# Two buffers for the splitting of weights in an mLSTM and feed-forward kernel, and a new place for the row gates' buffers

## The chip, the cores and the metric

The kernel runs on one core of a Trainium2 chip. The metric is the device time of one execution in microseconds (us). The engines are named as in the profile: PE (TensorE, matrix products), PEld (its weight loads), DVE (VectorE), ACT (ScalarE), POOL (GpSimd) and SP (SyncE, which here issues all DMAs).

## The reference

An mLSTM attention over B = 4, H = 8, S = 768, D = 40, whose output feeds a feed-forward layer of 320 to 2048 to 320 over 3072 tokens. Cut to what matters:

```python
for t in range(S):                                   # per batch and head
    m_new = max(f[t] + m, i[t])
    f_stab, i_stab = exp(f[t] + m - m_new), exp(i[t] - m_new)
    m = m_new
    C = f_stab * C + i_stab * outer(v[t], k[t])
    n = f_stab * n + i_stab * k[t]
    y[t] = sigmoid(o[t]) * (C @ q[t]) / max(abs(n @ q[t]), 1)
...
h = x @ w_in                                         # x: y as (3072, 320)
g = where(h >= 1, h, where(h <= -1, 0, (h + 1)**2 / 4))
out = g @ w_out
```

## The kernel before, in words

The sequence is cut into 6 chunks of 128 steps, so there are 24 pairs n of a chunk and a batch. For each pair a lower triangular matrix of decays A is built (an affine select on POOL, exponentials on ACT), multiplied into the scores k·q (DVE), and multiplied by v on PE; from the second chunk on, a carried state C is added (DVE tiles `hv`). The result y is transposed by PE into `xh` and `xl`, two parts of x.

The feed-forward layer works on 4 pairs (512 tokens) at a time, in 6 groups j, each with 16 slices fc of 128 of the 2048 hidden columns. For each slice `mm1` runs 8 products into one of two PSUM banks `psh`; ACT reads the bank into a tile `r` (a relu, then a square in place) and DVE reads the bank once more and finishes r (`scalar_tensor_tensor`, "the read r" in what follows). Only after that read may the bank be written for the slice after the next. `mm2` multiplies r into four banks `pso` two slices later. From j = 1 on, r is split into `gh` and `gl`, and w_out is split too.

The weights come as 64-bit numbers and are turned into 32-bit numbers on the chip, in 16 pieces: 8 of w_in (two slices each, 128 x 768 numbers, "in0" to "in7") and 8 of w_out (128 x 640, "out0" to "out7"), in the order in0, in1, out0, in2, out1 and so on. Raw words are loaded into `wraw`, which has two buffers; the load of the piece after the next is issued when the piece in its buffer has been read. `words` then does five steps: the *magnitude* (ACT, from wraw into `mg`), the *sign* (DVE, from wraw into the upper halves of the output), the *low half* (POOL, from wraw into the lower halves), the *clamp* (DVE, mg in place), and the *combine* (DVE, mg into the output). For w_in the output is the tile `win`, which is split further: its *high part* goes to `wh` (ACT) and its *rest* to `wl` (DVE). For w_out the output is a tile `ow`, and it is split only from j = 1 on (into `oh` and a second `ow`).

The time before the first feed-forward products is called the front; its order is written out by hand, one token a step (STEPS), and each engine keeps it. `c` in it converts in0, `d` its rest; `Lf`, `b` and `g1` load the row gates of four chunks, find their maxima and sum them on DVE (tiles `fi_r`, `m_r`, `fi_b`, `m_b`). Behind the front a planner, which plays the program through with estimated times while it is built, sets the order on each engine: it takes what is ready by its estimates and comes first in the program. A tile whose buffer is still in use isn't ready. What the code gives it for the pieces is this:

```python
while nw < min(len(W_ORDER), DUE(fc)):      # DUE(fc) = 3 + fc, group j = 0 alone
    split_next()
...
with behind((m, "act"), (m, "dve")):        # in split_next: not ahead of the last copy of xh, xl
    for _ in convert(*W_ORDER[nw]):
        pass
if nw + 2 < len(W_ORDER):
    load_w(*W_ORDER[nw + 2])
```

The memory is handed out in pools. `stage` holds wraw, win and mg; it is given back when the last piece is converted, and `late` (the tiles v3 and m3 of later pairs) takes its place. `gate` holds what only the front needs; at its end `gates.close()` gives it back, and `mo` (tiles r, gh, gl) takes its place. `mid` stays to the end.

Of the kernel before, what the change touches and what calls it, by code (L numbers as in the profile page):

```python
# [7 lines left out]
F32 = mybir.dt.float32  # L8
# [11 lines left out]
L = 128  # L20
# [3 lines left out]
P = 128  # L24
# [3 lines left out]
NSEQ = B * H  # L28
# [70 lines left out]
def mlstm_ffn_kernel(ctx, tc, qk, qn, vk, og, fi0, fi, fib, w_in, w_out, cst, out):  # L99
# [9 lines left out]
    stage = stages.enter_context(tc.tile_pool(name="stage", bufs=2, side="right"))  # L109
# [7 lines left out]
    mid = ctx.enter_context(tc.tile_pool(name="mid", bufs=1))  # L117
    gates = ExitStack()
    gate = gates.enter_context(tc.tile_pool(name="gate", bufs=1))
# [61 lines left out]
    mb = {}  # L181

    def load_batch():
        mb["row"] = mid.tile([NSEQ, 2, 4 * L], F32, name="fi_r")
        nc.sync.dma_start(mb["row"], fi[:, :, L:5 * L])
        mb["fi"] = mid.tile([P, 2, L], F32, name="fi_b")
        nc.sync.dma_start(mb["fi"], fib)

    def batch_maxima():
        m = mid.tile([NSEQ, 4 * L + 1], F32, name="m_r")  # L190
        nc.vector.tensor_copy(m[:, 0:1], carry)
        nc.vector.tensor_tensor_scan(out=m[:, 1:], data0=mb["row"][:, 0, :], data1=mb["row"][:, 1, :], initial=m[:, 0:1],
                                     op0=ALU.add, op1=ALU.max)
        nc.vector.tensor_copy(carry, m[:, 4 * L:])
        mb["m"] = mid.tile([P, L + 1], F32, name="m_b")
        for c in range(4):
            nc.sync.dma_start(mb["m"][c * NSEQ:(c + 1) * NSEQ], m[:, c * L:(c + 1) * L + 1])
# [174 lines left out]
    def words(out, raw):  # L372

        n = raw.shape[1] * raw.shape[2] // 2
        hi = raw.rearrange("p k (f w) -> p (k f) w", w=2)[:, :, 1]
        quarter = raw.rearrange("p k f -> p (k f)").bitcast(U16).rearrange("p (f w) -> p f w", w=4)
        out = out.rearrange("p k f -> p (k f)").bitcast(I32)
        halves = out.bitcast(U16).rearrange("p (f w) -> p f w", w=2)  # L380
        mg = stage.tile([P, n], F32, name="mg", bufs=1)
        nc.scalar.activation(mg, hi.bitcast(F32), AF.Abs, scale=65536.0)
        nc.vector.tensor_scalar(out=halves[:, :, 1], in0=quarter[:, :, 3], scalar1=0x8000, scalar2=None,
                                op0=ALU.bitwise_and)

        nc.gpsimd.tensor_scalar(out=halves[:, :, 0], in0=quarter[:, :, 1], scalar1=1 / 8192, scalar2=-4095.5 / 8192,
                                op0=ALU.mult, op1=ALU.add)
        nc.vector.tensor_scalar_max(mg, mg, TINY)
        nc.vector.scalar_tensor_tensor(out=out, in0=mg.bitcast(I32), scalar=3, in1=out,
                                       op0=ALU.logical_shift_left, op1=ALU.bitwise_or)  # L390

    def split(hi, lo, w):
        nc.scalar.copy(hi, w)
        yield
        nc.vector.tensor_tensor(out=lo, in0=w, in1=hi.bitcast(F32), op=ALU.subtract)
# [14 lines left out]
    def convert(kind, i):  # L410
        raw = raws.pop((kind, i))
        if kind == "in":
            sl = slice(2 * i * P, 2 * (i + 1) * P)
            w = stage.tile([P, 3, 2 * P], F32, name="win", bufs=1)
            words(w, raw)
            yield
            yield from split(wh[:, :, sl], wl[:, :, sl], w)
        else:
            of[i] = ow.tile([P, 656], F32, name="ow")[:, :2 * DM].rearrange("p (k e) -> p k e", k=2)
            words(of[i], raw)  # L420
            if 2 * i >= PLAIN_FC:
                yield
                yield from split_out(i)

    def split_out(i):
        w = of.pop(i)
        ol[i] = ow.tile([P, 656], F32R, name="ow")[:, :2 * DM].rearrange("p (k e) -> p k e", k=2)
        yield from split(oh[:, 2 * i:2 * i + 2, :], ol[i], w)
# [359 lines left out]
    def split_next(m="x"):  # L788
        nonlocal nw
        if nw < len(W_ORDER):  # L790
            with behind((m, "act"), (m, "dve")):
# [4 lines that stand above are left out]
            nw += 1  # L796
# [5 lines left out]
    for what in STEPS.split():  # L802
        n = int(what[1]) if what[1:2].isdigit() else 0
        hh = int(what[2:] or 0)
        if what == "Lg":
            first_gates()
        elif what == "Lf":
            load_batch()
        elif what == "Lc":
            nc.sync.dma_start(cs_t, cst[0:120, P:])  # L810
# [14 lines left out]
        elif what[0] == "g":  # L825
            if n:
                batch_sums()
            else:
                run(gate_sums(n))
        elif what[0] == "b":  # L830
            batch_maxima()
        elif what[0] == "k":
            run(gate_tail(n))
        elif what[0] == "h":
            gate_exps(n)
        elif what[0] == "A":
            add_sums(n)
        elif what[0] == "E":
            exponents(n)
        elif what[0] == "p":  # L840
            first_sums()
        elif what[0] == "v":
            scale1(n)
        elif what[0] == "o":
            sigmoid(0)
        elif what[0] == "x":
            decay(n, hh)
        elif what[0] == "c":
            rest = convert(*W_ORDER[nw])
            next(rest)  # L850
            load_w(*W_ORDER[nw + 2])
            nw += 1
        elif what[0] in "ed":
            next(rest, None)
        elif what[0] == "w":
            heat = int(what[1:])
        elif what[0] in "uytz":
            if what[0] == "u":
                mains[n] = main(n)
            next(mains[n])  # L860
# [110 lines left out]
```

## Time and profile before

| | |
|---|---|
| median of 3 runs | 518.3 us (518.03 to 519.18) |
| the profiled execution | 517.97 us, its span 516.2 us |
| PE busy | 490.7 us (95%) |
| DVE busy | 343.0 us (66%) |
| ACT busy | 289.1 us (56%) |
| POOL busy | 135.9 us (26%) |
| mean granted clock of PE | 0.979 |
| DMA | 51.48 MB, mean 100 GB/s |

The profile is of one execution. Its views are the page (busy time of each engine), the waits (which engine waited for whom, total, times and longest), the chain that ended last (followed back from the last instruction, step by step to what released it), the time line (start, duration, engine, line, operation, output and inputs with their shapes, and in brackets the idle time before it and what ended it), and the stretches (busy time of each engine in a stretch of time, the clock granted to PE as a share of full speed, and the use of the DMA engines). Nearly all instructions carry line 82 or 85, that of a helper, so they are told apart by their tiles.

### The profile page before, as it was taken

How to read it: one execution, taken by the hardware profiler on the slowest of the kernel's cores; microseconds unless marked ns; L12 is line 12 of the kernel's file. 1: busy time of each engine (PE TensorE's matmuls, PEld its weight loads, DVE VectorE, ACT ScalarE, POOL GpSimd, SP SyncE). 2: the span in 40 equal slices, each digit the busy share in tenths (PEclk: the TensorE clock that was granted, in tenths of full speed). 3: DMA queues.
4: the chain of work that ended last, by engine and by line, in shares of the span. 5: the costliest groups of instructions: out<-in, count | busy, mean ns of one | idle time of the engine just before them, and what ended most of it. 6: DMA issues, size and time to landing. Idle time of an engine off the chain costs nothing.

```text
span 516.2 us, 8817 instructions
## 1 busy us (share of the span) xinstructions
PE 490.7 (95%) x3396; PEld 419.4 (81%) x3399; DVE 343.0 (66%) x621; ACT 289.1 (56%) x560; POOL 135.9 (26%) x136
## 2 busy tenths in 40 slices
PE   8985999889898999999999998999999999999996
PEld 3763877778677989988889988889888889988986
DVE  4789896679758776759696657756756745444332
ACT  4525884436087555676645567555377554455553
POOL 2324531343433333323142314403230210000000
PEclk8987999979999999999999999999999999999999
DMA  8868664364441303323223423113522000010001
GB/s 227 257 183 307 161 189 138 115 193 150 131 146 40 107 27 96 118 66 111 65 78 83 133 80 118 68 53 96 170 81 77 16 1 1 0 52 1 1 2 51
DMA packets 29646, 51.48 MB, mean 100 GB/s; under 512 B 10060, under 2 KB 19940, under 8 KB 29604
## 3 DMA queue, kind: packets, MB, share of 16 engines
q1 hardware_dynamic: 29604, 50.92, 32.4%
q8 instruction: 27, 0.44, 0.4%
q14 instruction: 15, 0.12, 0.1%
HBM read 46.80 MB, written 4.04 MB: 98 GB/s over the span
## 4 chain that ended last, share of the span: by engine, by line
PE 85%; DVE 6%; ACT 5%; DMA 3%; issue 1%; SPq 0%; ACTq 0%; DVEq 0%
PE pso L82 33%; PE psh L82 33%; PE psa L82 15%; ACT Abc L82 1%; PE pso L85 1%; DMA raw<-in_qk 1%; ACT L82 1%; PE psa L85 1%; DVE ow L82 1%; DMA wraw<-in_w_in 1%; PE psh L85 1%; ACT r L82 1%; DVE win L82 1%; DMA out<-r 1%; ACT sig L82 0%
## 5 line engine op out<-in xcount | busy, mean ns | idle before, releaser
L82 ACT ACTIVATE r<-psh,half 128x512 f32<-128x512 f32 x96 | 65.4, 685 | 111.7 <-PE psh L82 111.4
L82 DVE SCALAR_TENSOR_TENSOR r<-psh,r 128x512 f32<-128x512 f32 x96 | 65.8, 686 | 71.5 <-ACT r L82 71.3
L82 PE MATMUL psh<-xh,wh 128*128 128x512 f32 x288 | 104.3, 418 | 6.7 <-DVE r L82 6.1
L82 PE MATMUL pso<-oh,gh 128*128 128x320 f32 x320 | 100.6, 317 | 2.4 <-ACT gh L82 2.1
L82 PE MATMUL psh<-xh,wl 128*128 128x512 f32 x288 | 99.8, 401 | 0.0
L82 PE MATMUL pso<-ow,gh 128*128 128x320 f32 x320 | 99.2, 312 | 0.0
L82 PE MATMUL pso<-oh,gl 128*128 128x320 f32 x320 | 94.0, 311 | 1.6 <-DVE gl L82 1.6
L82 DVE TENSOR_TENSOR gl<-r,gh 128x512 fp32r<-128x512 f32 x80 | 62.2, 779 | 40.5 <-ACT gh L82 40.4
L82 ACT CAST gh<-r 128x512 fp32r<-128x512 f32 x80 | 49.4, 618 | 51.0 <-DVE r L82 50.4
L82 PEld LDWEIGHTS pso<-oh,gh 128*128 128x128 f32 x320 | 60.1, 188 | 7.4 <-ACT gh L82 2.5
L82 PEld LDWEIGHTS psh<-xh,wl 128*128 128x128 f32 x288 | 55.2, 192 | 13.1 <-DVE wl L85 0.4
L82 PEld LDWEIGHTS psh<-xh,wh 128*128 128x128 f32 x288 | 51.8, 194 | 15.2 <-DVE r L82 6.8
L82 PEld LDWEIGHTS pso<-ow,gh 128*128 128x128 f32 x320 | 60.2, 188 | 2.8
L82 PE MATMUL psh<-xl,wh 128*128 128x512 f32 x192 | 62.3, 405 | 0.0
L82 ACT ACTIVATE r<-r 128x512 f32<-128x512 f32 x96 | 60.4, 632 | 2.5
L82 PEld LDWEIGHTS pso<-oh,gl 128*128 128x128 f32 x320 | 58.9, 188 | 2.1 <-DVE gl L82 1.9
L82 ACT ACTIVATE Abc<-Abc,nA 128x128 f32<-128x128 f32 x160 | 49.9, 391 | 0.2
L82 POOL TENSOR_TENSOR v<-vk,G 128x328 f32<-128x328 f32 x36 | 30.6, 856 | 58.3 <-issue 45.9
L82 PEld LDWEIGHTS psh<-xl,wh 128*128 128x128 f32 x192 | 36.8, 192 | 8.6
L82 PE MATMUL pso<-ow,r 128*128 128x320 f32 x128 | 38.5, 443 | 0.5 <-DVE ow L82 0.5
L82 POOL TENSOR_SCALAR_AFFINE_SELECT Abc<-Abc 128x1024 f32<-128x1024 f32 x20 | 25.4, 1275 | 48.3 <-DMA Abc<-a_d 46.1
L82 POOL TENSOR_TENSOR m<-m 128x1024 bf16<-128x1024 f32 x12 | 24.4, 2037 | 46.4 <-DVE m L82 46.4
(203 smaller groups left out, 681.0 us busy)
## 6 DMA issues: line engine op xcount, KB each, us to landing
Abc<-a_d SPq DMA_DIRECT2D x20, 512.0 KB
raw<-in_qk SPq DMA_DIRECT2D x48, 160.0 KB
vk<-in_vk SPq DMA_DIRECT2D x20, 324.0 KB
wraw<-in_w_in SPq DMA_DIRECT2D x8, 768.0 KB
wraw<-in_w_out SPq DMA_DIRECT2D x8, 640.0 KB
sig<-in_og SPq DMA_DIRECT2D x6, 640.0 KB
out<-r SPq DMA_DIRECT2D x24, 160.0 KB
qn<-in_qn SPq DMA_DIRECT2D x20, 180.0 KB
```

The source lines that it names most:

```text
L82: r = getattr(self.engine, name)(*args, **kwargs)
L85: r = getattr(self.engine, name)(*args, **kwargs)
```

## The change

`win` (3 KB a partition) and `mg` (3 KB) get two buffers each in `stage`, and the tiles `fi_r` (4 KB) and `m_r` (2 KB) move from the pool `mid`, which stays, to the pool `gate`, which the front gives back.

```diff
     def load_batch():
-        mb["row"] = mid.tile([NSEQ, 2, 4 * L], F32, name="fi_r")
+        mb["row"] = gate.tile([NSEQ, 2, 4 * L], F32, name="fi_r")
...
     def batch_maxima():
-        m = mid.tile([NSEQ, 4 * L + 1], F32, name="m_r")
+        m = gate.tile([NSEQ, 4 * L + 1], F32, name="m_r")
...
-        mg = stage.tile([P, n], F32, name="mg", bufs=1)
+        mg = stage.tile([P, n], F32, name="mg", bufs=2)
         nc.scalar.activation(mg, hi.bitcast(F32), AF.Abs, scale=65536.0)
...
-            w = stage.tile([P, 3, 2 * P], F32, name="win", bufs=1)
+            w = stage.tile([P, 3, 2 * P], F32, name="win", bufs=2)
             words(w, raw)
```

## The prediction

> **What bounds the kernel now.** I read the page first, then the waits of the whole span, then the chain that ended last, and last the time line around the one long idle stretch of the TensorE (PE).
>
> ```profile
> PE 490.7 (95%) x3396; PEld 419.4 (81%) x3399; DVE 343.0 (66%) x621; ACT 289.1 (56%) x560; POOL 135.9 (26%) x136
> ...
> PE psh L82 <- DVE r L82: 6.1, 1, 6.1
> ...
> PE psa L82 <- DVE hv L82: 2.4, 2, 1.8
> ```
>
> PE is busy for 490.7 of 516.2 us, so all that any change of waits can win is the 25.5 us in which it is idle, and the time in which its clock is halved after an idle stretch. One wait is 6.1 us of that: PE waits for the VectorE's (DVE) last read of a psh bank. The two buffers that the change doubles, win and mg, only matter where such a stall runs through the splitting of weights (14 to 135 us). The chain that ended last, from its answer for 30 to 53 us, says how this stall comes about:
>
> ```profile
> 35.47 0.45 DVE ow L82
> 35.91 1.32 DVE mg L82
> 37.23 0.53 DVE win L82
> ...
> 37.89 4.31 DMA wraw<-in_w_in
> ...
> 42.30 0.60 DVE win L82
> 42.90 1.53 DVE ow L82
> ...
> 44.46 0.70 DVE r L82
> ...
> 45.20 3.78 PE psh L82 x8
> ```
>
> Read it upward: PE restarts at 45.20, behind the DVE's read "r". That stands behind the combine of piece out0 and the sign of piece in2, which waited until 42.2 for in2's load. The load could start only at 37.89, when the last reader of the raw buffer it overwrites was through: the DVE's sign of piece in1 ("win"), which stood behind out0's sign and in1's clamp ("mg").
>
> **The change part by part.** It issues no instruction or DMA more and none less; it takes away waits for buffers, and the planner may then order each engine anew. I cost it at the stall, with the time line of DVE, ACT and POOL there (start, duration):
>
> ```profile
> 34.30 0.96 DVE L85 TENSOR_TENSOR wl<-win,wh 128x768 fp32r<-128x768 f32 x1
> 35.18 0.28 DVE L85 TENSOR_TENSOR fi_b<-fi_b,m_b 128x128 f32<-128x128 f32 x1
> 35.81 1.43 DVE L82 TENSOR_SCALAR mg<-mg 128x768 f32<-128x768 f32 x1
> 37.15 0.60 DVE L82 TENSOR_SCALAR win<-wraw 128x768 uint16<-128x768 uint16 x1
> 38.38 1.49 DVE L82 SCALAR_TENSOR_TENSOR win<-mg,win 128x768 int32<-128x768 int32 x1
> 42.79 1.64 DVE L82 SCALAR_TENSOR_TENSOR ow<-mg,ow 128x640 int32<-128x640 int32 x1
> 46.48 0.55 DVE L82 TENSOR_SCALAR mg<-mg 128x768 f32<-128x768 f32 x1
> 47.76 0.94 DVE L82 SCALAR_TENSOR_TENSOR win<-mg,win 128x768 int32<-128x768 int32 x1
> ...
> 33.41 0.91 ACT L82 ACTIVATE mg<-wraw 128x768 f32<-128x768 f32 x1
> 39.90 0.83 ACT L82 CAST wh<-win 128x768 fp32r<-128x768 f32 x1 [5.59 <-DVE win L82]
> 40.64 0.79 ACT L82 ACTIVATE mg<-wraw 128x640 f32<-128x640 f32 x1
> 41.33 1.24 ACT L82 ACTIVATE r<-psh,half 128x512 f32<-128x512 f32 x2
> 42.47 1.14 ACT L82 ACTIVATE r<-r 128x512 f32<-128x512 f32 x2
> ...
> 32.36 0.91 POOL L82 TENSOR_SCALAR ow<-wraw 128x640 uint16<-128x640 uint16 x1 [12.36 <-DMA wraw<-in_w_out]
> 35.41 1.41 POOL L82 TENSOR_SCALAR win<-wraw 128x768 uint16<-128x768 uint16 x1 [2.13 <-issue]
> ```
>
> *Second win.* In1 now waits until in0's rest (34.30 + 0.96 = 35.26) has left the one win. POOL shows it: its part of in1 starts at 35.41, right behind, though it had nothing to do from 33.27. With two buffers in1's sign needs only its raw words, so I put it at 35.47, ahead of clamp and of out0's sign. It ends at 36.07, and with the 0.13 us from its end to the load (37.23 + 0.53 to 37.89) in2's load goes out at 36.20 in place of 37.89: 1.69 us sooner. Landing after the same 4.31 us, at 40.5, it no longer holds anybody. POOL's part can run in the 12.36 us in which POOL sat idle before 32.36, so in1's clamp no longer runs beside it: 0.55 us (the row at 46.48) in place of 1.43, less 0.88.
>
> *Second mg.* Out0's magnitude (0.79) now follows in1's combine on ACT at 40.64; with a buffer of its own it fits into ACT's idle 5.59 us. So the two activations of r start behind "wh" alone. In1's combine, at 35.47 + 0.60 (sign) + 0.55 (clamp) + 0.28 (fi_b) = 36.9, plus 1.49, ends at 38.4; wh at 39.2; two activations of r at 40.5; the first square (half of 1.14) at 41.1. The read "r" is then ready at 41.1 in place of 43.0.
>
> *What is late next* is the DVE's own queue. From 35.47 to 44.46 it has 9.0 us of work with no hole over 0.1; less 0.88 the same work ends at 43.6. So the read starts between 41.1 (nothing ahead of it that isn't needed) and 43.6 (all is still ahead of it): a gain of 3.4 to 0.9 us. I take the 1.7 us by which the chain's load moves (start at 42.8), since it is the step that the chain names; it means that in2's sign (0.60), which comes after r in the program, falls behind the read. Below, the gain can be used up where the planner puts more of in2 ahead (a rival).
>
> The next rows are of the waits, the stretches (columns: length, busy time of PE, PEld, DVE, ACT and POOL, granted clock, DMA share, GB/s), and the time line of DVE and of SP's queue.
>
> ```profile
> POOL win L82 <- DVE wl L82: 7.4, 3, 3.3
> ...
> 44.00:50.50 6.50, 5.30 (x12) 3.94 (x13) 6.04 (x14) 2.58 (x5) 3.35 (x3) 0.50 1.02 352
> 46.00:94.00 48.00, 48.00 (x232) 36.98 (x231) 38.24 (x58) 30.26 (x59) 19.07 (x18) 0.95 0.61 184
> ...
> 134.32 1.10 DVE L82 SCALAR_TENSOR_TENSOR ow<-mg,ow 128x640 int32<-128x640 int32 x1
> 137.90 0.49 DVE L82 TENSOR_TENSOR v<-v 128x328 f32<-128x328 f32 x1
> ...
> 26.48 3.97 SPq L85 DMA_DIRECT2D m_b<-m_r  x4
> ```
>
> *What the rest of the span does with it.* Later pieces lose waits too (7.4 us of POOL's for win), but PE has no idle time between 46 and 94 us, so these are worth nothing; if PE were not busy there they would be worth up to those 7.4 us. A PE that runs ahead by 1.7 us at 45 keeps it as long as it stays the bound. Weight loads go out earlier, into a stretch in which the DMA engines are full (share 1.02 from 44 to 50.5); nobody on PE's path waits for them but the order of pieces, so 0, and up to one load's 4.31 us delayed by sharing if a piece falls behind its products.
>
> *Row gates' buffers into the front's pool.* Nothing is issued differently. The first r, which lies where that pool lay, now waits also for fi_r and m_r. Their last readers are the four copies of m_r issued from 26.48 to 30.45, and what they brought is read at 35.18 (fi_b row); the first r is written at 41.33, or 39.2 by my sum. So this wait is over 4 us before it counts: 0; were it not covered it would delay r one for one. A wait or two more ahead of that r is inside the rounding. The pool that is opened where the doubled buffers lay has its first use at 137.90 (v), after the last combine (134.32 + 1.10): 2.5 us of slack, 0.
>
> **Sum.** −1.7 us. The profiled execution took 517.97 us (span 516.2), 0.33 under the median of 518.3; I take the difference from the median: 516.6 us.
>
> **The clock.** Two more stretches show, with the one from 44 to 50.5, what a stall costs beyond its idle time:
>
> ```profile
> 34.00:37.00 3.00, 3.00 (x8) 1.98 (x8) 2.97 (x5) 0.31 (x1) 1.41 (x1) 0.52 1.03 379
> 40.00:44.00 4.00, 0.00 (x0) 0.00 (x0) 3.81 (x8) 3.61 (x6) 1.45 (x1) 0.96 0.72 250
> ```
>
> After the stall PE works 5.3 us at half clock, a loss of 2.65 us. If the cold time moves along with the restart, the sum stands. Cold stretches here last 3.0 or 6.5 us, so they come in steps of about 3.3. [...]
>
> **Rivals.** (1) *The clock comes back a step sooner.* For it: the cold stretch after 34 us took one step, this one two, and PE restarts close to an edge (43.5 against 44). Against: the phase may differ in each run. It gives 3.3 / 2 = 1.65 us more: 515.0.
>
> (2) *The queue is the bound and hides it.* DVE has no hole from 34 to 44.5, so if the planner keeps all of the same work ahead of the read, only the 0.88 us stay, and PE's early restart runs at half clock up to the same edge, which halves them: 517.9. POOL's early part can also fall beside the front's DVE work, as fi_b and combines do beside POOL in these rows. [...]
>
> (3) *Slower: pieces run ahead of what PE waits for.* The one mg kept the next piece's clamp and combine behind the last. With two, they can be ready while the planner's DVE waits for something that PE needs. The place is PE's second stall behind splitting:
>
> ```profile
> 104.18 1.37 DVE L82 SCALAR_TENSOR_TENSOR win<-mg,win 128x768 int32<-128x768 int32 x1
> 105.47 0.49 DVE L82 TENSOR_TENSOR hv<-psa,hv 128x328 f32<-128x328 f32 x1
> 107.43 0.44 DVE L82 TENSOR_SCALAR mg<-mg 128x640 f32<-128x640 f32 x1
> 108.79 1.02 DVE L82 SCALAR_TENSOR_TENSOR ow<-mg,ow 128x640 int32<-128x640 int32 x1
> ```
>
> PE waits 1.8 us for "hv" (waits view) at 105.47, already behind one combine; the next clamp and combine, now later, cost 1.46 us if put ahead. By the same mechanism in2's pair (0.55 + 0.94 = 1.49) and its sign (0.60) take the gain at 42.8. Together 518.3 + 1.5 = 519.8. It decides where out's magnitude is ready before hv's matmuls end. Against: hv comes first in the program.
>
> **How the numbers follow.** Forecast 516.6: 0.38 (its own range, from the gains of 3.4 and 0.9 us, 514.9 to 517.4; nearly all of it is over 0.2%). Rival 1, 515.0: 0.17. Rival 2, 517.9: 0.24. Rival 3, 519.8: 0.21. About 0.2% (1.04 us) is what a measurement can tell here: the forecast and rival 1 are faster (0.55), rival 2 same (0.24), rival 3 slower (0.21). The range goes from the read at its earliest (3.4 us) with the clock's step partly won, 513.8, to rival 3 with a little more, 520.0.
>
> **What would show it.** Right: in1's sign ahead of its clamp on DVE; POOL's part of in1 before 32 us; in2's load at about 36.2; out0's magnitude right behind in1's on ACT; the read at about 42.8 and PE's wait for it near 4.4 us; the half clock after it as long as now. Rival 1 shows in the granted clock from 47 us. Wrong: a load still near 37.9; a combine of in2 ahead of the read; hv later than 105.5 less the lead; a new wait of ACT's r for fi_r or m_r.

## The result and the profile after

After the change the kernel takes 523.5 us (median; 523.07 to 524.44) against 518.4 us for the kernel before on the same chip: a ratio of 1.0102, 95% interval 1.0085 to 1.0119. The forecast was 516.6 with a range up to 520.0. The change costs 5.1 us where 1.7 us were to be won. Here and below, medians in us are of all executions of a kernel, and the ratios leave out single executions over 1.5% slower than its fastest.

The page of the kernel after, and its waits of PE and of DVE (columns: who waited for whom, us in total, times, the longest):

```profile
span 522.0 us, 8816 instructions
PE 493.3 (94%) x3396; PEld 421.2 (81%) x3399; DVE 342.8 (66%) x621; ACT 288.7 (55%) x560; POOL 135.8 (26%) x136
```

```profile
PE psh L82 <- DVE r L82: 9.4, 3, 5.5
PE psa L82 <- DVE hv L82: 2.3, 2, 1.7
...
DVE win L82 <- DMA wraw<-in_w_in: 5.1, 2, 3.3
```

PE waits three times for the read r, 9.4 us in all, where it waited once for 6.1. The wait for hv, at which the prediction had looked for a loss, is as it was. The profiled span has grown by 5.8 us (522.0 against 516.2). In 3.2 of them PE is idle (28.7 against 25.5), and in 2.6 it is busy (493.3 against 490.7) with the same 3396 matmuls, because it works at half clock for longer (by the stretches the granted clock was 0.50 for 27.3 us in place of 20.5). And DVE, which had no such wait before, stands still for 5.1 us until two loads of w_in have landed. Its time line has the first of them ahead of the first read (here and below: start, duration, engine, line, operation, out<-in, and in brackets the idle time before and what ended it):

```profile
34.53 0.60 DVE L82 TENSOR_SCALAR win<-wraw 128x768 uint16<-128x768 uint16 x1
...
35.42 0.95 DVE L82 TENSOR_SCALAR mg<-mg 128x768 f32<-128x768 f32 x2
...
40.82 0.61 DVE L82 TENSOR_SCALAR win<-wraw 128x768 uint16<-128x768 uint16 x1 [1.82 <-DMA wraw<-in_w_in]
41.32 1.23 DVE L85 TENSOR_TENSOR_SCAN ac_b<-rst,ah_b 128x128 f32<-128x128 f32 x1
...
42.65 1.60 DVE L82 TENSOR_TENSOR wl<-win,wh 128x768 fp32r<-128x768 f32 x1
44.28 0.69 DVE L82 SCALAR_TENSOR_TENSOR r<-psh,r 128x512 f32<-128x512 f32 x1
...
72.73 0.63 DVE L82 TENSOR_SCALAR win<-wraw 128x768 uint16<-128x768 uint16 x1 [3.30 <-DMA wraw<-in_w_in]
73.23 1.38 DVE L82 TENSOR_SCALAR mg<-mg 128x640 f32<-128x640 f32 x1
...
76.47 1.54 DVE L82 TENSOR_TENSOR wl<-win,wh 128x768 fp32r<-128x768 f32 x1
77.93 0.68 DVE L82 SCALAR_TENSOR_TENSOR r<-psh,r 128x512 f32<-128x512 f32 x1
```

In1's sign runs at 34.53, ahead of the clamps, as forecast, and so in2's load goes out early. But the next sign of win, in2's, has moved up as well: the planner has a free second win, takes in2's load for done, and puts the sign ahead of a scan, the rest of in1 and the first read, which were all ready by 39.4. In DVE's time line they come behind it: the scan starts at 41.32, the rest at 42.65 and the read at 44.28. (That the planner takes the load for done is my reading of the order; its estimates are not in the trace.) In the kernel before, this sign stood ahead of the first read too, but behind the scan and the rest of in1. ACT had squared the first slice by 39.4:

```profile
38.79 0.63 ACT L82 ACTIVATE r<-r 128x512 f32<-128x512 f32 x1
```

At 72.73 the same happens with in5: ACT has squared the seventh slice by 71.7, but DVE waits 3.30 us for in5's load, and out3's clamp and combine, two steps of the decays and in4's rest (`wl`) stand ahead of the seventh read as well. The third wait is that for the thirteenth read, which stands behind out6's clamp and combine and in7's rest. PE's own time line has the second and the third:

```profile
78.66 0.73 PE L82 MATMUL psh<-xh,wh 128*128 128x512 f32 x2 [1.57 <-DVE r L82]
...
129.26 0.73 PE L82 MATMUL psh<-xh,wh 128*128 128x512 f32 x2 [2.29 <-DVE r L82]
```

Counted from the start of slice 0 (the first slice of 128 columns), the kernel after is 1.4 us ahead of the kernel before at slice 6 (32.4 against 33.8), 3.1 us behind at slice 8 (46.0 against 42.9), 4.9 at slice 12 and 6.3 at the last. So in these two executions the loss arises behind slice 6; the first stall, 5.5 us against 6.1, is a gain that did not come.

The loads themselves: in2's goes out 0.5 us ahead of out1's and takes 5.53 us, against 4.31 before (chain that ended last). In5's goes out at 66.82 and lands after 5.88 us. It had to wait for the last reader of its buffer, in4's magnitude on ACT, which stands behind 20 decays (time lines of ACT and of SP's queue):

```profile
35.27 5.53 DMA wraw<-in_w_in
```

```profile
65.86 0.91 ACT L82 ACTIVATE mg<-wraw 128x768 f32<-128x768 f32 x1
...
61.91 0.36 SPq L82 DMA_DIRECT2D wraw<-in_w_out  x1
66.82 0.36 SPq L82 DMA_DIRECT2D wraw<-in_w_in  x1
```

So the theory for the experiments was (T1): *the loss is the order that the planner makes with the second buffers; steps of a later piece that wait for a load stand ahead of reads, squares and hv.* Against it: the second buffers cost by themselves, by earlier loads that collide (T2), or the move of the row gates' buffers does (T3).

### The profile page after: what moved, and what is told of

It is laid out like the page before. It is cut to its first block, busy times and chain, and to the rows that moved or that the text cites. A ratio compares the mean times of both kernels' runs of the same rounds, so it can differ in the third digit from the quotient of the medians.

```text
span 522.0 us, 8816 instructions
## 1 busy us (share of the span) xinstructions
PE 493.3 (94%) x3396; PEld 421.2 (81%) x3399; DVE 342.8 (66%) x621; ACT 288.7 (55%) x560; POOL 135.8 (26%) x136
## 4 chain that ended last, share of the span: by engine, by line
PE 73%; DVE 10%; ACT 6%; DMA 6%; issue 2%; POOL 2%; SPq 0%; ACTq 0%; DVEq 0%; POOLq 0%
PE pso L82 30%; PE psh L82 30%; PE psa L82 13%; DMA wraw<-in_w_in 2%; ACT Abc L82 1%; DMA Abc<-a_d 1%; DVE win L82 1%; DVE ow L82 1%; ACT r L82 1%; ACT L82 1%; DMA sig<-in_og 1%; ACT Abc L85 1%; DMA wraw<-in_w_out 1%; DVE r L82 1%; POOL Abc L82 1%
## 5 line engine op out<-in xcount | busy, mean ns | idle before, releaser
L82 PE MATMUL pso<-oh,gh 128*128 128x320 f32 x320 | 100.5, 316 | 2.4 <-ACT gh L82 2.2
L82 PE MATMUL psh<-xh,wl 128*128 128x512 f32 x288 | 101.3, 405 | 0.0
L82 PE MATMUL pso<-oh,gl 128*128 128x320 f32 x320 | 95.7, 313 | 1.0 <-DVE gl L82 1.0
L82 PE MATMUL pso<-ow,r 128*128 128x320 f32 x128 | 41.1, 462 | 0.2 <-DVE ow L82 0.2
L82 POOL TENSOR_SCALAR_AFFINE_SELECT Abc<-Abc 128x1024 f32<-128x1024 f32 x20 | 23.8, 1196 | 49.8 <-DMA Abc<-a_d 46.9
```

The source lines that it names most:

```text
L82: r = getattr(self.engine, name)(*args, **kwargs)
```

## The experiments

Slices are counted from 0, reads from the first. Several runs hold the engines to a chosen order: the program is built once to have the planner's order, and built again with every instruction tied, without a semaphore, behind the one that comes before it in the chosen order on its engine. In the diffs `one` is the planner's order for one buffer each, `two` that for two. Each ratio is to the kernel before on the same chip, with its 95% interval.

### The parts of the change

**The move alone**

```diff
+ mb["row"] = gate.tile(..., name="fi_r")        # mid before
+ m = gate.tile(..., name="m_r")                 # mid before
  ... mg and win: bufs=1
```

> Only the row gates' buffers (fi_r, m_r) move to the pool that the front gives back; mg and win keep one buffer. Every engine's planned order is that of the kernel before. T1 (the second buffers cost, because the planner puts later pieces' steps ahead of the reads): 518.4 us, within 0.5. T3 (the move costs: the row gates wait for the front's buffers): up to the whole 5.1 us, 523.5, with the row gates' load or ACT's relus waiting in the trace.

518.61 us, 1.0003 (0.9974 to 1.0032). No cost is seen, and by the interval it is 1.7 us at most, not 5.1; T3 falls.

**Two buffers, the old order**

```diff
+ plan = order of the program with bufs=1       # every engine held to it
  mg = stage.tile(..., bufs=2);  w = stage.tile(..., name="win", bufs=2)
```

> The whole change, but every engine is held to the order that the planner made for the one-buffer kernel (two buffers, the order of before). T1 (the planner's new order is what costs): 518.4 us within 1, first stall of PE 6 us as before, no stall near 77 us. T2 (the second buffers cost whatever the order is, by loads that go out at other times or by clashes of accesses): 522 to 524, with the stall near 77 us and the loads of 5.5 to 5.9 us.

517.03 us, 0.9983 (0.9960 to 1.0007). T2 falls: the whole change in the old order loses nothing, and the difference to the kernel after, 6.5 us by the medians and 6.2 by the ratios, is in the order alone. The holding itself is not what makes it fast: orders that are held in the same way lose 5 us in two runs below. DVE and PE at the first stall of this run:

```profile
39.99 0.61 DVE L82 TENSOR_SCALAR win<-wraw 128x768 uint16<-128x768 uint16 x1
40.48 1.63 DVE L82 SCALAR_TENSOR_TENSOR ow<-mg,ow 128x640 int32<-128x640 int32 x1
42.15 0.69 DVE L82 SCALAR_TENSOR_TENSOR r<-psh,r 128x512 f32<-128x512 f32 x1
...
42.90 1.22 PE L82 MATMUL psh<-xh,wh 128*128 128x512 f32 x2 [3.89 <-DVE r L82]
```

In2's sign stands ahead of the read here too, but behind the scan and the split, and doesn't wait: the load is there. PE restarts 2.3 us sooner than before (42.90 against 45.20): 1.2 us is a front that was earlier in this run (slice 0 began at 32.35 against 33.56), and 1.1 us is the read. The stall itself, 3.89 us where 6 were expected, is 2.2 us shorter than before also because PE took 1.1 us longer for its first two slices.

**One of the two buffers**

```diff
  win: bufs=2, mg: bufs=1                        # e3
  win: bufs=1, mg: bufs=2                        # e4
```

> Two buffers for win, one for mg. In the planned order of VectorE the sign of in2 is ahead of the clamp and combine of out0 and these ahead of the first read, so by T1 the first stall stays: in2's load lands about 40.8, plus 0.61, 1.3 and 1.4 makes the first read 44.1 (before 44.46); the seventh read is ahead of in5's sign, so no stall near 77. T1: 517.5 to 519.5 us. If win's second buffer alone carries the cost (the sign that waits for a load in VectorE's queue): 523.

> Two buffers for mg, one for win. In the planned order the first read is ahead of the high-low split of in1 and of every sign that waits for a load, so by T1 it comes at about 41 (before 44.46) and the first stall shrinks from 6.1 to 3 us or less; the second read is behind the sign of out1 and its square behind out1's magnitude, as after, and the seventh square behind out3's magnitude, so some of it can come back near 77. T1: 514 to 520, point 517. If mg's second buffer carries the cost (ACT's magnitudes that wait for a load ahead of the squares): 522 to 524 with both stalls of after.

Two for win alone: 520.26 us, 1.0050 (1.0024 to 1.0076), 0.8 us above the expected band. The first stall stayed (5.75 us), as expected, and slice 12 came no later after slice 0 than before (74.1 us against 74.5); the loss comes behind it and I did not trace it further (the profiled execution, 518.67 us, is the fastest of the twelve and shows only part of it). Two for mg alone: 517.12 us, 0.9985 (0.9963 to 1.0007), with the read at 40.83, as expected, and a first stall of 3.9 us where 3 or less were expected. The planner's answer differs with every combination; neither buffer carries the loss alone.

### Where the order loses

**The order of after in the front only, and behind the front only**

```diff
  plan = two[: fourth read] + rest of one        # e5
  plan = one[: fourth read] + rest of two        # e6
```

> Two buffers each; every engine is held to the planner's order for two buffers up to and with the fourth read, and from there to its order for one buffer. If the loss arises behind the front, in the stretch from 60 to 135 us (T1: in the traces the fifth slice stands 0.1 us later after than before, once the front's own 0.85 is taken off, and the later ones 5 to 6): 517 to 518.5. If it arises in the front, where the loads of in2 and out1 go out together and take 5.5 us, and is only seen later: 521 to 524.

> The reverse: the order for one buffer up to and with the fourth read, from there that for two. T1 with the loss behind the front: 521 to 523.5, with PE's new stalls near 77 and 127 us. With the loss in the front: 517 to 518.5.

523.30 us, 1.0103 (1.0069 to 1.0136), and 523.85 us, 1.0103 (1.0074 to 1.0132). Each half alone costs all of it; I had expected one or the other. In the first, in2's load took 6.75 us and the read came at 46.56 (chain that ended last):

```profile
36.32 6.75 DMA wraw<-in_w_in
...
46.56 0.70 DVE r L82
```

and PE waited 7.18 us, then 1.75 us more from 69.5 for the fifth read, which in before's order stands behind ACT's 16 decays. After's own order has the fifth square ahead of these decays and so wins back at slice 6 what its front lost: there slice 6 begins 32.4 us after slice 0, in before 33.8. What it loses comes later.

**That part in two**

```diff
  plan = one[: tenth read] + rest of two                             # e10, the tail
  plan = one[: fourth read] + two[.. tenth read] + rest of one       # e11, the middle
```

> Two buffers, the order of before up to and with the tenth read (84 us), from there the order of after, in which the clamps and combines of in6, out5, in7 and out6 stand ahead of hv and of the thirteenth read. With the losses of the run with the order of after from the fourth read on (523.85) put down to places: stalls there of 1.97 and 2.94 us for hv and the thirteenth read, against 1.77, 0.80 and 0.49 in before's order: 1.9 us of it here, and cold clock behind them: 519 to 521. If the middle (slices 4 to 9) carries it all: 516.5 to 518.

> Two buffers, the order of before, but for the stretch from the fifth to the tenth read, which is in the order of after. If that stretch's stalls (1.33 and 0.98 us for the fifth and seventh read in the run with the order of after from the fourth read on) are the loss: 519 to 521; with the tail as its only place: 516.5 to 518. If the parts add up, this and the run with the order of after in the tail alone together lose 6 us to the run with the order of before throughout (517.03).

519.29 us, 1.0022 (1.0003 to 1.0041), and 521.57 us, 1.0063 (1.0038 to 1.0088), the latter 0.6 above the expected band. Against the old order (517.03) the tail costs 2.3 us and the middle 4.5 us; together 6.8, as much as both in one run (523.85 − 517.03 = 6.8). By the ratios it is 2.0, 4.1 and 6.2 us, each with an uncertainty of about 2 us. Within that the losses behind the front add up.

**After, with one instruction moved**

```diff
  plan = two, but DVE: sign of in2 behind the first read
```

> The order of after on every engine, but for one instruction: VectorE's sign of in2 stands behind the first read and not ahead of the scan, the split of in1 and that read. If this sign's wait for its load is what makes the first read late (T1), the read starts near 40.8 (after: 44.28) and the first stall falls from 5.5 to about 2 us. What becomes of it: if the gain carries, 519 to 520; if, as in the run with the first two reads moved ahead, slice 6 takes it back (there 4.7 us of 6.6 were gone by slice 6), 522 to 524.

521.98 us, 1.0082 (1.0053 to 1.0110). PE's time line:

```profile
41.09 0.82 PE L82 MATMUL psh<-xh,wh 128*128 128x512 f32 x2 [2.23 <-DVE r L82]
...
123.66 1.22 PE L82 MATMUL psh<-xh,wh 128*128 128x512 f32 x2 [3.49 <-DVE r L82]
```

The read started at 40.34 and the stall is 2.23 us, as forecast from the sign's wait: this part of T1 is shown. In the whole time it is worth little, 1.5 us of 5.1 by the medians, and the intervals of the two ratios overlap. The profiled execution, the fastest of its eight with 519.69 us, shows where the rest goes: slice 12 begins 73.9 us after slice 0, no later than before (74.5) and 5.5 us sooner than after (79.4), but slice 16 stands at 112.7 against 109.4 before, behind the last stall, which has grown to 3.49 us. The second and third stalls I did not take away one by one; that they come from the order of the pieces rests on the two runs above.

**A rule in place of an order**

```diff
- split_next()
+ split_next("r" if x else "x")      # behind the last read and square
```

> After, with one line changed: from the second slice on a piece is planned behind the last read and square, in place of the last copy of x. The planner then still chooses its order, but no sign stands ahead of a read of two slices earlier; the pieces' steps run ahead up to in7, in front of hv. T1: the first read is ahead of in2's sign though behind in1's split, 42 or so; 514 to 518. If running ahead by itself costs (hv behind the last pieces): 520 to 523.

520.36 us, 1.0038 (1.0019 to 1.0058): the second case. The first stall is 2.5 us, but the planner now does slices 12 to 15 ahead of the attention of the next chunk (slice 12 begins 64.4 us after slice 0, in before 74.5), and PE then waits for y, C and decays (2.35, 1.22 and less), its mean granted clock over the run is 0.970 (before 0.979), and at slice 34 it is 3.7 us behind. Not ahead of a read is not enough for a rule.

### What the second buffers are worth in a good order

**Two reads ahead of the pieces, with two buffers and with one**

```diff
  plan = one, but
    ACT: out0's magnitude, relu 0, square 0, in1's high part, relu 1, square 1
    DVE: ..., out0's clamp, in1's and out0's combines, read 0, in1's rest, scans, read 1, in2's sign
  # e7: bufs=2.  e13: bufs=1, out0's steps behind in1's combine
```

> Two buffers and the order of before, but for the stretch of the first two reads: ScalarE squares the first slice ahead of in1's high part, and VectorE makes the first read ahead of in1's split, of the scans and of in2's sign. In the trace of the run with two buffers in the old order PE waits 3.89 us for this read (it ends at 42.8) and its third slice then runs at half clock until 50 us. T1 (a read is late because pieces stand ahead of it): the read ends near 39, the stall is under 0.7 us, the half clock does not come, and 4 to 6 us are gained: 511 to 514. If the pieces' loads bound the front, the stall moves to the fifth slice or its products and 1 us at most is gained: 516 to 517.5.

> The order with the first two reads ahead (517.54 with two buffers), with one buffer each for mg and win: out0's magnitude, clamp and combine then come behind in1's combine, and so behind the first read, the rest stands as it was. If the gain is the order's, and the second buffers add nothing (T1): 516.5 to 518.5. If the second buffers carry it (out0's combine late for the first products, the next loads late): 519 to 521.

Two buffers: 517.54 us, 0.9988 (0.9963 to 1.0013). The stall is gone and the half clock with it (granted clock 1.00 from 40 to 100 us), and slice 3 begins at 44.99, in the run with the old order at 49.33; but PE then waits for the fifth read (PE and ACT of this run):

```profile
40.66 0.71 PE L82 MATMUL psh<-xh,wh 128*128 128x512 f32 x2 [0.17 <-DVE r L82]
...
65.51 0.72 PE L82 MATMUL psh<-xh,wh 128*128 128x512 f32 x2 [1.99 <-DVE r L82]
```

```profile
56.31 4.79 ACT L82 ACTIVATE Abc<-Abc,nA 128x128 f32<-128x128 f32 x16
...
63.13 0.63 ACT L82 ACTIVATE r<-r 128x512 f32<-128x512 f32 x1
```

Its matmuls had ended at 53.5; its square stands in ACT's queue behind 16 decays. I had put 511 to 514. Against the run with the old order the lead is 5.7 us at slice 3 and 1.0 at slice 6; this wait, and one of 1.28 us for out1's combine, took most of it.

One buffer each, in the same order: 521.63 us, 1.0061 (1.0032 to 1.0090). This is 4.1 us slower than with two (3.8 by the ratios), against my expectation that the buffers add nothing. Out0's magnitude can then only follow in1's combine, out1's load goes out at 45.23 and not at 42.82, and DVE and PE wait (time lines):

```profile
50.11 0.53 DVE L82 TENSOR_SCALAR ow<-wraw 128x640 uint16<-128x640 uint16 x1 [3.01 <-DMA wraw<-in_w_out]
...
51.53 0.33 PE L82 MATMUL psa<-ident,fi_b 128*128 128x128 f32 x1 [2.71 <-DVE fi_b L82]
```

So the second buffers are worth 4 us, in an order that was made for two; the best order for one buffer was not looked for.

**The same manner onwards**

```diff
  plan = e7's, but up to the eighth read
    ACT: relu and square 4 ahead of 20 of the 24 decays, relu and square 5 ahead of 10
    DVE: in2's combine ahead of out1's sign; reads 2 to 7 ahead of the signs that wait
```

> The run with the first two reads ahead, and in the same manner onwards: the combine of in2 ahead of out1's sign, the fifth slice's relu and square ahead of 14 of the 16 decays, in5's sign behind the seventh read and out3's combine. In the run with two reads ahead the seventh slice began at 65.51 because ScalarE had 16 decays (4.79 us), a high part and a magnitude ahead of the fifth square (63.13). If the order of VectorE's and ScalarE's queues is all that holds it: slice 6 begins near 62, the stalls of 1.28 and 1.99 us go, and 511 to 514.5 us come out, faster than both kernels. If loads hold the pieces (the full DMA stretch of 48 to 56 us): within 1 us of that run, 516.5 to 518.

516.36 us (515.3 for the six executions in the ratio), 0.9952 (0.9923 to 0.9980): faster than both kernels, but short of the 511 to 514.5 that I expected. The wait for the fifth read is gone, that for out1's combine is not (1.56 us), and slice 6 begins 28.7 us after slice 0 (33.8 before). Of these 5.1 us, 3.5 are left at slice 12 (70.9 against 74.5) and 2.8 at the last slice.

**And in6 and out5 ahead of hv; and the loads of in7 and out6 earlier**

```diff
  plan = e12's, but                               # e14
    DVE: signs, clamps and combines of in6 and out5 in its idle stretches ahead of the 12th read
    ACT: their magnitudes and in6's high part ahead of the 12th relu
  # e15: and SP: loads of in7 and out6 ahead of qn and of the decays' load; in7's steps earlier
```

In both, the pieces are no longer held behind the last copy of x.

> The run with reads ahead of the pieces (516.36), and in6 and out5 converted before hv: their signs, clamps and combines go into VectorE's idle stretches between 85 and 94 us (in that run's trace both loads have landed by 84.7), in6's high part ahead of the decays, so that hv waits for no piece. There hv comes at 103.16 behind a sign, a clamp and a combine of in6, PE waits 1.77 us, and the granted clock is then 0.96, 0.50 and 0.68 in three stretches of 4 us. If the wait goes and the clock stays up: 1.5 and up to 3.4 us less, 511 to 514. If the clock drops there for another reason than this wait: 514.5 to 515.5. If the earlier pieces make another read or hv late: 516 to 518.

> As the run before, and in7 and out6 too: their loads go out right behind the buffers' release at 86 and 88 us and not at 100.57 and 104.87, and in7 is converted ahead of the thirteenth read. PE has no stall between 105.7 and 129 in the trace, so this should be worth 0 to 0.5 us against the run before; more would mean that pieces late there are covered by work that is itself moved.

The first: 515.27 us, 0.9924 (0.9895 to 0.9953), the lowest median; its interval overlaps that of the run before. The second hv waits only for its matmuls now, and PE for it 0.18 us where it waited 1.77. The clock dropped nevertheless, so the middle of the three cases came (DVE and PE of this run, then its stretches: length, busy time of PE, PEld, DVE, ACT, POOL, granted clock, DMA share, GB/s):

```profile
101.77 0.50 DVE L82 TENSOR_TENSOR hv<-psa,hv 128x328 f32<-128x328 f32 x1 [1.60 <-PE psa L82]
...
102.32 1.01 PE L82 MATMUL psa<-raw 40*128 40x128 f32 x6 [0.18 <-DVE hv L82]
```

```profile
98.00:100.00 2.00, 1.21 (x10) 0.99 (x9) 1.85 (x5) 0.61 (x2) 1.21 (x2) 1.00 0.76 219
100.00:102.00 2.00, 2.00 (x18) 1.91 (x17) 0.40 (x2) 0.00 (x0) 0.32 (x2) 1.00 0.81 228
102.00:104.00 2.00, 1.82 (x16) 1.68 (x14) 1.46 (x5) 0.00 (x0) 0.60 (x1) 0.54 0.90 282
```

This trace also shows a second limit. Its order is that of the run before up to the twelfth read, but in3's load came late, DVE waited 3.65 us for it and PE 2.31 us from 55.8, and slice 6 began 31.4 us after slice 0, not 28.7. There it is a load that holds the pieces, and no longer their order.

The second: 518.91 us, 1.0000 (0.9974 to 1.0027). The earlier loads lose all of it. They stand ahead of the decays' load in SP's queue. That load goes out at 89.47 and POOL begins with it 6.3 us later, at 95.82; in e14 it went out at 90.00 and took 3.8 us (93.82). ACT's decays start late, and with them come late the copy of x that stands behind them and the last part of x, which DVE has at 100.5 (POOL, ACT and PE of this run; PE restarts 0.15 us behind that part here and in e14, and the profile puts the wait down to the magnitude that ends at the same time):

```profile
95.82 1.09 POOL L82 TENSOR_SCALAR_AFFINE_SELECT Abc<-Abc 128x1024 f32<-128x1024 f32 x1 [5.56 <-DMA Abc<-a_d]
...
96.95 2.45 ACT L82 ACTIVATE Abc<-Abc,nA 128x128 f32<-128x128 f32 x8 [1.73 <-POOL Abc L82]
99.30 0.45 ACT L82 CAST xh<-psa 128x384 fp32r<-128x384 f32 x1
...
100.67 3.60 PE L82 MATMUL psa<-v,Abc 128*128 128x41 f32 x16 [1.90 <-ACT mg L82]
```

I had priced these loads at 0 to 0.5 us of gain: the mistake of the prediction once more.

## Why the prediction was wrong

In short: the gain of 1.7 us did not come, because the planner put in2's sign, waiting for its load, ahead of the first read. The loss of 5.1 us came from the order of the pieces behind the front, which the prediction had put at 0.

- *Second win, second mg: what moves.* Right, as far as the steps that it names: in1's sign ahead of the clamps, POOL's part of in1 at 22.07 in place of 35.41, in2's load at 35.27 (forecast 36.20), out0's magnitude right behind in1's. Slice 0 began 0.85 us sooner in this run, so the load moved by 1.8 us against slice 0, as forecast (1.69).
- *"In2's sign ... falls behind the read."* Wrong, and this is the step that failed first. The load moved as was forecast, but the planner moved the sign that reads it by more, ahead of a scan and a split that it had stood behind. It is program order against estimated readiness: the prediction took the program's order for the planner's. The read came at 44.28, not 42.8, and counted from slice 0 that is 0.7 us later than before (11.6 against 10.9); with the order held it came 1.1 us sooner than before (42.15, its slice 0 at 32.35, against 44.46 and 33.56), so the 1.69 us of the sum were somewhat large even there.
- *"Landing ... it no longer holds anybody"* and *"nobody on PE's path waits for them but the order of pieces, so 0."* Wrong. The load took 5.53 us (6.75 in the run with after's order in the front only) in place of 4.31, and DVE waited 1.82 us for it in front of the read. In both, out1's load was out 0.5 us behind it, but with two buffers for win alone, where out1's load followed 4.1 us later, it took 5.32, so what lengthens it is not shown. Moving that one instruction behind the read made the stall 2.23 us in place of 5.50.
- *"PE has no idle time between 46 and 94 us, so these are worth nothing."* It is right that nothing can be won there, but not that nothing can be lost: the new order of the middle costs 4.5 us and that of the tail 2.3 us when they come alone.
- *Rival 3, pieces run ahead of what PE waits for* (0.21), is the mechanism that came. Its place and price were off: it named hv at 105.47, where the wait stayed at 1.7 us, and 1.5 us net. PE now waits at three reads (5.50, 1.57 and 2.29 us; the first is no longer than before), and the loss is 5.1 us.
- *The clock.* "If the cold time moves along with the restart, the sum stands": it did not quite at the first stall (PE restarted at 45.0, and its clock was back by 49.1, 1.4 us sooner than before, where it restarted at 45.2), and behind the second came a cold stretch that was not there before (stretches after, the same columns as above; before, all three had 1.00):

```profile
76.00:80.00 4.00, 2.00 (x10) 1.38 (x9) 4.00 (x7) 1.30 (x2) 1.43 (x2) 0.98 0.58 197
80.00:84.00 4.00, 4.00 (x11) 2.81 (x10) 3.91 (x6) 2.05 (x3) 1.51 (x2) 0.59 0.51 164
...
112.00:116.00 4.00, 4.00 (x9) 2.83 (x9) 3.58 (x6) 0.00 (x0) 2.62 (x3) 0.50 0.55 197
```

  At 0.59 PE did 4 × 0.41 = 1.6 us less work in those 4 us. The last row is of the half clock behind hv: it ended at about 112 before and at about 117.4 after, which is 10.2 us of it in place of 6.8.

  In all, the half clock lasted 3.41, 6.83 or 10.24 us at a time in these two traces (stretches of 0.5 us; before: 9.56 to 12.97, 33.45 to 36.86, 43.69 to 50.52 and 105.13 to 111.96 us; after: 32.07 to 38.90, 42.31 to 49.14, 79.86 to 83.27 and 107.16 to 117.40). So the steps of rival 1 are there, though of 3.4 us and not 3.3. At the first stall there were two of them in both, in the run with the old order two again (about 6.9 us) and in the tail run, whose order is the same up to there, one (about 3.4). That an earlier restart saves one, which 515.0 and the lower end of the range, 513.8, count on, no run shows, and the edge that rival 2 holds fixed lay at 50.52 before and at 49.14 after.
- *Row gates' buffers: 0.* Right (1.0003).
- *The range.* Its upper end, 520.0, was rival 3 with little more. What was priced at 0 "if the order stays" had no bound of its own, though the text said that "the planner may then order each engine anew".

What stays open: that the front's order and the rest's do not add up beyond slice 6 I put down to the place of the fifth square, which I read in the orders and did not test alone; what makes in2's load longer; which step of the pieces makes the second and third stalls; and the 1.9 us that win's second buffer costs behind slice 12 when it comes alone.

## What to carry to other kernels

A second buffer does two things: it takes a wait away, and it gives whoever orders the queues more to put early. Where a planner with estimated loads does the ordering, price the second as well: list every queue on which a step that waits for a load could now stand ahead of a step that the bound engine waits for. Hold the order fixed to see what the buffer itself is worth (here a ratio of 0.9983 in the old order, and 4 us in an order made for it), and let steps run ahead into idle stretches of their engine, not ahead of a read; and a load sent early is not free when a needed load queues behind it (in the last run the decays' load then took 6.3 us and not 3.8).

What two buffers are worth can be told only with the order named: 517.5 us with two against 521.6 with one in one order, 523.5 against 518.4 in those that the planner made.

## What the runs showed of the hardware

In two of the traces the clock fell without a long wait. In e14 PE's waits between 96 and 102.5 us were 0.58, 0.31, 0.48 and 0.18 us, and the granted clock was 0.54 right behind (rows above); the stretch is full of short matmuls (128x41 and 120x123; 10 in the 2 us from 98 and 18 in those from 100). In the kernel after, the clock fell behind the waits of 0.42 and 1.57 us that ended at 78.66 (0.59, rows further up). Behind the 1.99 us from 63.52 in e7 it did not fall:

```profile
64.00:68.00 4.00, 2.49 (x10) 1.99 (x11) 3.13 (x6) 3.99 (x11) 0.00 (x0) 1.00 0.79 196
68.00:72.00 4.00, 4.00 (x17) 3.03 (x16) 3.37 (x6) 3.51 (x5) 1.27 (x1) 1.00 0.67 220
```

So in these traces the length of a single wait does not decide it: in e14 the clock fell behind waits of 0.58 us at most, in e7 it did not behind one of 1.99. What does, these runs do not settle.

The front, up to slice 0 nearly the same instructions in all versions, took from 32.1 to 34.8 us to that slice in the profiled runs; where the half clock falls in it differs from run to run (before from 9.56 to 12.97 us, after nowhere ahead of 32.07). The distance from slice 0 to a later slice takes this out: it is 470.9 and 471.2 us to the last slice for the kernel before and for the move alone. It has a spread of its own, though: in orders that are the same up to there, slice 6 stands 1.1 us apart in the run with the old order and in the tail run, and 2.7 us apart in the run with the same manner onwards and in e14. Differences of that size between single traces, this document's too, are not safe.
